# Where a pair's state products are issued, and GpSimd's order in the second pair

## The chip, the cores and the metric

The kernel runs on one core of a Trainium2 chip. The metric is the device time of one execution, in microseconds; times given for a kernel are medians over its runs. A core has TensorE (PE, matrix products into PSUM), VectorE (DVE), ScalarE (ACT), GpSimd (POOL) and SyncE (SP, which here only issues DMAs). Each engine works through its own list of instructions in order; semaphores make one engine wait for another.

## The reference, cut to what matters

Two blocks, one behind the other. The first is a state-space layer (Mamba-2's chunked form) over 4 sequences of 768 tokens with 8 heads of 32 channels and a state of 16; the second is a two-layer feed-forward block on the 3072 x 256 result, with 2048 hidden units and a parametric ReLU.

```python
for c in range(nc):
    L = np.exp(cum[:, :, :, None] - cum[:, :, None, :]) * causal
    M = np.einsum('bhin,bhjn->bhij', Cc, Bc) * L
    y_intra = np.einsum('bhij,bhjd->bhid', M, xc)
    y_inter = np.einsum('bhin,bhnd->bhid', Cc, state) * decay_to_i[:, :, :, None]
    y[:, :, sl] = y_intra + y_inter
    Bx = np.einsum('bhjn,bhjd->bhjnd', Bc, xc) * decay_from_j[:, :, :, None, None]
    state = decay_full[:, :, None, None] * state + np.sum(Bx, axis=2)
...
h = x @ w_in
g = np.maximum(h, 0.0) + alpha * np.minimum(h, 0.0)
return (g @ w_out).astype(np.float32)
```

The two weight matrices arrive as 64-bit floats; the kernel turns them into 32-bit floats itself, in pieces of 256 columns (`convert_a`, `convert_b`, `convert`).

## The kernel before, in words

**Pairs and groups.** The 24 chunks of 128 tokens are taken two at a time: 12 pairs, numbered 0 to 11. Two pairs make a group of 512 tokens, so there are 6 groups, and the feed-forward block works on groups. While the quads of group g run, pairs 2g + 2 and 2g + 3 are computed for the next group.

**A pair** is a Python generator (`pair`, L418); each call of `ssm(gp)` (L917) lets it issue its next stage. Its steps are: transposes of B and C (L511) and ScalarE's copy of them (`bc`); the decays, by scans on DVE (`half_decays`, L438, and `decays`, L427); C spread for the heads (`spread_c`, ScalarE) and C times the running decay (`c_decayed`, L528, POOL, tile `cd`); the state additions `added` (L473, PE, L478); the new states `states` (L483: DVE L490, then the heads' mask on POOL, L493, tile `sm`); the Gram products of B and C (`products_bc`, L573, PE, L580), in four strips r of 32 rows that run side by side, two of them into `ss` tiles and, for r = 2 and 3, into the two `hp` tiles; the multiplication of decays and Gram products on DVE (L614; in pairs 0 and 1 two heads of it are done by POOL, `times`, L591); the outputs (L633 and L640, PE); and two copies of them on ScalarE (L649). Pairs from 4 on are called fine: their scans and products are cut into more stages. B is scaled ahead by POOL (`pair_loads`, L379, tile `bn`).

**Quads.** Groups 1 to 5 use a scheme with seven half-size products in place of eight, in both layers. A group has four quads, z = 0 to 3, and there are 20 quads, i = 0 to 19 (`quad`, L773). A quad computes hidden units in two `hp` tiles, A and Y, by seven products (L785), each of two instructions and so four rows of the trace: A1, Y1, A2, Y2 and so on, in this order: A (copied by ScalarE to m1), Y (copied to m5), A again (copied to u2), then A, Y, then A for g21 and, last, Y for g11. Before the last one ScalarE copies m1 into Y (L814), after g12 was read from it. The parametric ReLU (`prelu`, L764) is a ScalarE product (L768) and a DVE maximum (L770). POOL then forms differences of the blocks (L819, L828). Between its products a quad calls `after(j)`, steps j = 1 to 14, and all else is hung into these steps by tables: the stages of the pairs (`steps`), the output products (`product`, L749, PE L760, numbered 1 to 7, each of four rows and of two halves of two) of the quad before it, combining a finished group's products (`combine`, L837), sums of weights (`weight_sums`, L728), and B's scaling for coming pairs. Even quads (z = 0 and 2) that have a pair beside them hold the Gram products in step 13; odd ones hold the outputs in step 5. The first quad (i = 0) has no output products of a quad before it, and in their place those of group 0 (L699).

**Before the quads.** Pairs 0 and 1 are computed alone; from about 30 us on, group 0 goes through the feed-forward block in the plain way (`hidden`, L656, `output`, L693) while pairs 2 and 3 are computed and the weights are converted. `slopes` (L306, POOL, L308 to L317) derives the factors of the parametric ReLU, and `hidden_two` (L668) starts group 0's hidden units with half a group.

The order on every engine is the program's order, written out by hand: `manual_schedule` takes it as it stands, and tile pools set which buffer is reused.

Of the kernel before, what the change touches and what calls it, by code (L numbers as in the profile page):

```python
# [22 lines left out]
def kernel(  # L23
# [25 lines left out]
    nc = tc.nc  # L49
# [279 lines left out]
    beside = {}  # L329

# [87 lines left out]
    def pair(gp):  # L418
# [4 lines left out]
        fine = gp >= 2 * GC // 2  # L423
# [43 lines left out]

        nk = 1 if last else 2
        st = [masked.get(b)]
        new = work.tile([P, 2, P], F32, name="state")  # L470
        sm = work.tile([P, 2, P], F32, name="sm")

        def added(dps):  # L473
            dps = dps[:, : 2 * Q].rearrange("p (k m) -> p k m", m=P)
            for k in range(nk):
                for w in range(KC):
                    ws = slice(64 * w, 64 * w + 64)
                    nc.tensor.matmul(dps[ws, k], bn[:, k, ws], xt[:, k, w * P : (w + 1) * P],  # L478
                                     start=True, stop=True, tile_position=(0, 64 * w),
                                     skip_group_check=True)  # L480
            return dps

        def states(dps):  # L483
            for k in range(nk):
                old = state.get(b)
                if old is None:
                    nc.scalar.copy(out=new[:, k], in_=dps[:, k])
                else:
                    e = (k + 1) * Q - 1
                    nc.vector.scalar_tensor_tensor(out=new[:, k], in0=old, scalar=pf[:, e : e + 1],  # L490
                                                   in1=dps[:, k], op0=ALU.mult, op1=ALU.add)
                state[b] = new[:, k]
            nc.gpsimd.tensor_tensor(out=sm[:, :nk], in0=new[:, :nk],  # L493
                                    in1=hmask.unsqueeze(1).to_broadcast([P, nk, P]), op=ALU.mult)
            st.extend(sm[:, k] for k in range(nk))
            masked[b] = st[-1]

        if fine:
            bn = bns.pop(gp) if gp in bns else pair_loads(gp)
            dps = added(beside.pop(gp) if gp in beside else ss_tile()[:, : 2 * Q])  # L500
            yield
            states(dps)
            yield


# [25 lines left out]

        if gp < 2:
            spread_c()
# [6 lines left out]
        if not fine:  # L540
            bn = bns.pop(gp) if gp in bns else pair_loads(gp)
# [6 lines left out]

        if fine:
            for k in range(2):  # L550
                for w in range(2):
                    half_decays(k, w)
                    if k == 1 and w == 1:
                        spread_c()
                        c_decayed()
                    yield
        else:
            if gp > 1:
                states(added(ss_tile()))
                c_decayed()  # L560
            decays(0)
            if gp == 1:
                dps = added(dps)
            if gp:
                yield
            if gp != 1:
                decays(1)
            if gp > 1:
                spread_c()
# [30 lines left out]
        elif gp == 1:  # L600
            gram = products_bc()
            g0 = one_less(gram)
            yield
            decays(1)
            states(dps)
            times(dec[:, :, :2], g0)
        else:
            if not fine:
                yield
            gram = products_bc()  # L610
# [11 lines left out]
        ys = [ss_tile() for w in range(KC)]  # L622
        y = [t[:, : 2 * Q].rearrange("p (k t) -> p k t", k=2) for t in ys]
        if fine:
            beside[gp + 1] = ys[1][:, 2 * Q :]
# [17 lines left out]
        if fine:  # L643
            yield
# [104 lines left out]
    def product(g, z, n, parts=(0, 1)):  # L749

        if g not in ms:
# [4 lines left out]
        for p in parts:  # L756
# [212 lines left out]
    ssm(1)  # L969
    slopes(alpha)  # L970
    ssm(1)
    prelus = [hidden_two(0, 0, 0, spare())]
    convert_next(first=False)
# [17 lines left out]
    for f in range(FIRST, NF):  # L991
# [12 lines left out]
        if f == 14:  # L1004
            bns[4] = pair_loads(4)
# [7 lines left out]
        if f in in_steps:  # L1013
# [3 lines left out]
    ssm(2 * GC // 2, 4)  # L1017


    steps = {(0, 1): 0, (0, 2): 0, (0, 5): 0, (0, 13): 0, (1, 1): 0, (1, 5): 0,  # L1020
             (1, 12): 1, (1, 14): 1, (2, 1): 1, (2, 2): 1, (2, 5): 1, (2, 13): 1,
# [12 lines left out]

    with_gram = {5: ((1,), (2, (0,))), 7: ((2, (1,)), (3,)), 8: ((5, (0,)),), 11: ((5, (1,)), (7,)),
                 13: ((6,),), 14: ((4,),)}
    without = {3: ((1,),), 5: ((2,),), 7: ((3,),), 8: ((5,),), 9: ((7,),), 13: ((6,),), 14: ((4,),)}
    for i in range(NZ * (NG - 1)):
# [3 lines left out]
        def after(j, g=g, z=z, i=i, nxt=nxt):  # L1042
            places = with_gram if nxt < NP and z % 2 == 0 else without
            for n in places.get(j, ()) if i else ():
                product(*divmod(NZ + i - 1, NZ), *n)
# [7 lines left out]
            if g > 1 and z == 0 and j in (7, 11, 13, 14):  # L1053
                if j == 7:
                    comb[0] = combine(g - 1)
# [3 lines left out]
            if nxt + steps.get((z, j), NP) < NP:  # L1059
                ssm(nxt + steps[z, j])  # L1060

                if j == 5 and z % 2:
                    for p in (1, 0, 1):
                        if nxt + z // 2 + p < NP:
                            ssm(nxt + z // 2 + p)
            if nxt < NP and (z, j) == (3, 7):
                token_sums(g + 1)
            ahead = nxt + {(0, 9): 1, (2, 9): 2}.get((z, j), NP)
# [42 lines left out]
```

## Time and profile before

| | |
|---|---|
| time, median of 4 runs | 373.26 us (372.25 to 373.66) |
| profiled execution, its own time | 373.12 us |
| profiled execution, span of the core | 371.0 us |
| PE busy | 363.7 us |
| DVE, ACT, POOL busy | 246.1, 179.5, 201.2 us |
| TensorE clock granted | 1.0 |

The page of a profile gives each engine's busy time, the chain of work that ended last, and the costliest groups of instructions. A row of a timeline has the start in us, the length in us, the engine, the line of the program, the operation, its tiles (written <- read), its shape and how many instructions were merged (x8); in brackets, how long the engine had been idle and what ended that. A wait list has engine, tile and line, whom it waited for, and then the sum in us, the number and the longest. PE rows overlap: a 128x256 row is 0.38 us long, and the next starts 0.216 us after it.

### The profile page before, as it was taken

The numbers are of one execution on the slowest core, as the hardware profiler recorded it, in microseconds if no ns is written. First come the engines' busy times: TensorE is split into PE (matmuls) and PEld (weight loads), VectorE is DVE, ScalarE is ACT, GpSimd is POOL, SyncE is SP. The second block draws the span as 40 slices with busy tenths as digits, with TensorE's granted clock in tenths as the row PEclk, the third lists the DMA queues.
The fourth block names the chain that finished last, engine by engine and source line by source line (L and its number), as shares of the span: only waits on it lengthen the run. The fifth ranks groups of instructions, "written<-read, shape, count | busy, mean of one in ns | idle before, by whom it ended". The sixth has DMA issues, their size and how long they took to land.

```text
span 371.0 us, 6171 instructions
## 1 busy us (share of the span) xinstructions
PE 363.7 (98%) x2223; PEld 292.0 (79%) x2223; DVE 246.1 (66%) x462; ACT 179.5 (48%) x384; POOL 201.2 (54%) x211
## 2 busy tenths in 40 slices
PE   8989999999999999999999999999999999999996
PEld 7766666578788888788788788788788788888884
DVE  7897979968448647838638738638747644643364
ACT  2647866436345345444444545446436425553541
POOL 4875566779738755725636526437445345264512
PEclk9999999999999999999999999999999999999999
DMA  8889999902175301004603702801801001001004
GB/s 163 178 166 317 266 269 220 193 10 58 42 143 103 82 3 57 2 0 74 140 3 58 155 2 48 167 0 35 177 3 29 2 0 28 4 0 30 0 0 85
DMA packets 121877, 30.71 MB, mean 83 GB/s; under 512 B 93736, under 2 KB 117752, under 8 KB 121848
## 3 DMA queue, kind: packets, MB, share of 16 engines
q1 hardware_dynamic: 116736, 29.74, 35.8%
q10 hardware_dynamic: 5112, 0.59, 1.1%
q8 instruction: 17, 0.28, 0.3%
q14 instruction: 12, 0.10, 0.1%
HBM read 26.98 MB, written 3.34 MB: 82 GB/s over the span
## 4 chain that ended last, share of the span: by engine, by line
PE 92%; DVE 2%; DMA 2%; POOL 1%; ACT 1%; issue 0%; ACTq 0%; POOLq 0%
PE hp L785 34%; PE bank L760 33%; PE bank L699 7%; PE hp L661 6%; PE ss L640 3%; PE ss L580 2%; PE ss L633 2%; PE ss L478 1%; PE ss L511 1%; PE hp L676 1%; DMA raw<-in_moe_w_in_dram 1%; DMA nat<-in_B_dram 1%; DVE dec L435 1%; PE bank L580 1%; PE bank L640 1%; DVE gt L770 0%
## 5 line engine op out<-in xcount | busy, mean ns | idle before, releaser
L828 POOL TENSOR_TENSOR gt<-gt 128x512 f32<-128x512 f32 x58 | 73.6, 1270 | 38.3 <-DVE gt L770 31.6
L760 PE MATMUL bank<-gt,w_out 128*128 128x256 f32 x320 | 82.4, 381 | 0.0
L770 DVE SCALAR_TENSOR_TENSOR gt<-hp,s_mul,gt 128x256 f32<-128x256 f32 x120 | 52.5, 479 | 43.5 <-ACT gt L768 40.8
L768 ACT ACTIVATE gt<-hp,s_alpha 128x256 f32<-128x256 f32 x120 | 50.3, 470 | 48.8 <-PE hp L785 36.6
L760 PEld LDWEIGHTS bank<-gt,w_out 128*128 128x128 f32 x320 | 60.1, 190 | 10.4 <-issue 2.3
L760 PE MATMUL bank<-gt,ws 128*128 128x256 f32 x240 | 59.5, 379 | 0.0
L819 POOL TENSOR_TENSOR gt<-gt 128x512 f32<-128x512 f32 x20 | 25.4, 1271 | 57.0 <-DVE gt L770 56.6
L760 PEld LDWEIGHTS bank<-gt,ws 128*128 128x128 f32 x240 | 45.1, 190 | 5.8
L441 DVE TENSOR_TENSOR_SCAN dec<-abc,bank 128x256 f32<-128x256 f32 x80 | 48.0, 660 | 0.0
L785 PE MATMUL hp<-xs,w_in 128*128 128x256 f32 x160 | 42.3, 387 | 0.0
L785 PE MATMUL hp<-xT,w_in 128*128 128x256 f32 x160 | 41.9, 384 | 0.1
L785 PE MATMUL hp<-xs,ws 128*128 128x256 f32 x160 | 40.7, 382 | 0.0
L793 ACT COPY m<-hp 128x512 f32<-128x512 f32 x20 | 11.7, 586 | 52.5 <-PE hp L785 47.4
L804 DVE TENSOR_TENSOR hp<-hp,u 128x512 f32<-128x512 f32 x20 | 13.9, 693 | 34.5 <-ACT u L802 34.5
L785 PEld LDWEIGHTS hp<-xT,w_in 128*128 128x128 f32 x160 | 29.1, 190 | 7.2 <-ACT hp L814 2.9
L785 PEld LDWEIGHTS hp<-xs,ws 128*128 128x128 f32 x160 | 29.8, 190 | 5.5 <-issue 1.1
L785 PEld LDWEIGHTS hp<-xs,w_in 128*128 128x128 f32 x160 | 29.3, 190 | 6.1 <-issue 1.2
L699 PE MATMUL bank<-w_out,gt 128*128 128x256 f32 x128 | 31.0, 384 | 0.0
L699 PEld LDWEIGHTS bank<-w_out,gt 128*128 128x128 f32 x128 | 23.7, 190 | 6.6 <-issue 3.7
L493 POOL TENSOR_TENSOR sm<-state,bmask 128x256 f32<-128x256 f32 (+1 forms) x12 | 7.8, 654 | 35.2 <-DVE state L490 35.0
L661 PE MATMUL hp<-xT,w_in 128*128 128x512 f32 x48 | 22.8, 597 | 0.2 <-DVE gt L688 0.2
L770 DVE SCALAR_TENSOR_TENSOR gt<-c,s_mul,gt 128x256 f32<-128x256 f32 x40 | 20.7, 559 | 0.0
(156 smaller groups left out, 550.2 us busy)
## 6 DMA issues: line engine op xcount, KB each, us to landing
abc<-z SPq DMA_DIRECT2D x20, 512.0 KB, 4.8
raw<-in_moe_w_in_dram SPq DMA_DIRECT2D x8, 512.0 KB, 5.6
raw<-in_moe_w_out_dram SPq DMA_DIRECT2D x8, 512.0 KB, 6.3
xt<-in_x_dram SPq DMA_DIRECT2D x24, 128.0 KB, 2.7
out_dram<-o_sb SPq DMA_DIRECT2D x32, 64.0 KB, 1.9
nat<-in_B_dram SPq DMA_DIRECT2D x22, 64.0 KB, 3.5
nat<-in_C_dram SPq DMA_DIRECT2D x22, 64.0 KB, 2.8
ap<-pf SPq DMA_DIRECT2D x11, 128.0 KB
```

The costliest lines, as they stand in the source:

```text
L441: nc.vector.tensor_tensor_scan(out=dv[:, k, hs], data0=abc[k][:, hs], data1=ident_p[0], initial=0.0, op0=ALU.mult, op1=ALU.add)
L640: nc.tensor.matmul(y[w][32 * q : 32 * q + 32, k], xt[:, k, h * D : (h + 1) * D], dec[:, k, h], start=False, stop=True, tile_position=(0, 3 ...
L661: nc.tensor.matmul(hp, w_in[:, k, f * P : (f + 1) * P], xts[g][:, k], start=(k == 0), stop=(k == KC - 1))
L699: nc.tensor.matmul(pos[0][t // 2][:, t % 2], gt[:, t * Q : (t + 1) * Q], w_out[:, f], start=(f == 0 and t % 2 == 0), stop=(f == NF - 1), s ...
L760: nc.tensor.matmul(ms[g][i][:, h], w, blocks[g, z][n][:, p], start=(q == 0 and h == 0), stop=(q == NQ - 1), skip_group_check=True)
L768: nc.scalar.mul(o[:, p], h[:, p], s_alpha[:, fs[p]])
L770: nc.vector.scalar_tensor_tensor(out=o[:, p], in0=h[:, p], scalar=s_mul[:, fs[p]], in1=o[:, p], op0=ALU.mult, op1=ALU.max)
L785: nc.tensor.matmul(to[:, p], w(2 * z + p), b, start=start and p == 0, stop=True, skip_group_check=True)
L793: nc.scalar.copy(out=m1, in_=A)
L804: nc.vector.tensor_tensor(out=Y, in0=Y, in1=u2, op=ALU.add)
L819: nc.gpsimd.tensor_tensor(out=tc_, in0=g22, in1=g12, op=ALU.subtract)
L828: eng.tensor_tensor(out=o, in0=x0, in1=x1, op=ALU.subtract)
```

## The change

Nothing is added to the computation or taken from it; instructions change places.

- In fine pairs the state additions (L478) and the states (L490, mask L493) were stages of their own at the head of a pair, called in the step of an odd quad that also has the outputs of the pair before (step 5). Their result went beside that pair's outputs, into the second half of a `ss` tile, and the outputs' copies were a stage behind. Now they are the stage before the Gram products, which a new entry of `steps` calls in step 9 of the even quad, into a `ss` tile of their own; `cd` is computed with them rather than with the last scans; and the copies follow the outputs at once.
- In even quads with a pair, product 1 goes back from step 5 to step 3, product 2 stands whole in step 5, 3 in step 7, 5 whole in step 8, and 7 in step 11.
- `combine` takes steps 5, 9, 13, 14 rather than 7, 11, 13, 14. B's scaling is called in steps (1, 3) and (3, 8) rather than (0, 9) and (2, 9), and pair 4's in its own first stage. Pair 4 has two stages ahead of the first quad rather than four.
- In pair 1, POOL's `times` goes ahead of `states`, and the third stage of the pair and the conversion of the second weight piece (whose last part is POOL's addition, L261) go ahead of `slopes`.

```diff
-        if fine:
-            bn = bns.pop(gp) if gp in bns else pair_loads(gp)
-            dps = added(beside.pop(gp) if gp in beside else ss_tile()[:, : 2 * Q])
-            yield
-            states(dps)
-            yield
...
         if fine:
             for k in range(2):
                 for w in range(2):
                     half_decays(k, w)
                     if k == 1 and w == 1:
                         spread_c()
-                        c_decayed()
                     yield
...
             decays(1)
+            times(dec[:, :, :2], g0)
             states(dps)
-            times(dec[:, :, :2], g0)
         else:
-            if not fine:
-                yield
+            if fine:
+                states(added(ss_tile()))
+                c_decayed()
+            yield
             gram = products_bc()
...
-        ys = [ss_tile() for w in range(KC)]
-        y = [t[:, : 2 * Q].rearrange("p (k t) -> p k t", k=2) for t in ys]
-        if fine:
-            beside[gp + 1] = ys[1][:, 2 * Q :]
+        y = [ss_tile()[:, : 2 * Q].rearrange("p (k t) -> p k t", k=2) for w in range(KC)]
...
-        if fine:
-            yield
         g, q = divmod(2 * gp, GC)
...
     ssm(0)
     ssm(1)
+    ssm(1)
+    convert_next(first=False)
     slopes(alpha)
-    ssm(1)
     prelus = [hidden_two(0, 0, 0, spare())]
-    convert_next(first=False)
     ssm(1)
...
-        if f == 14:
-            bns[4] = pair_loads(4)
...
-    ssm(2 * GC // 2, 4)
+    ssm(2 * GC // 2, 2)
-    steps = {(0, 1): 0, (0, 2): 0, (0, 5): 0, (0, 13): 0, (1, 1): 0, (1, 5): 0,
-             (1, 12): 1, (1, 14): 1, (2, 1): 1, (2, 2): 1, (2, 5): 1, (2, 13): 1,
+    steps = {(0, 1): 0, (0, 2): 0, (0, 5): 0, (0, 9): 0, (0, 13): 0, (1, 1): 0, (1, 5): 0,
+             (1, 12): 1, (1, 14): 1, (2, 1): 1, (2, 2): 1, (2, 5): 1, (2, 9): 1, (2, 13): 1,
              (3, 1): 1, (3, 5): 1, (3, 12): 2, (3, 14): 2}
...
-    with_gram = {5: ((1,), (2, (0,))), 7: ((2, (1,)), (3,)), 8: ((5, (0,)),), 11: ((5, (1,)), (7,)),
-                 13: ((6,),), 14: ((4,),)}
-    without = {3: ((1,),), 5: ((2,),), 7: ((3,),), 8: ((5,),), 9: ((7,),), 13: ((6,),), 14: ((4,),)}
+    with_gram = {3: 1, 5: 2, 7: 3, 8: 5, 11: 7, 13: 6, 14: 4}
+    without = {3: 1, 5: 2, 7: 3, 8: 5, 9: 7, 13: 6, 14: 4}
...
-            if g > 1 and z == 0 and j in (7, 11, 13, 14):
-                if j == 7:
+            if g > 1 and z == 0 and j in (5, 9, 13, 14):
+                if j == 5:
                     comb[0] = combine(g - 1)
...
-                if j == 5 and z % 2:
-                    for p in (1, 0, 1):
-                        if nxt + z // 2 + p < NP:
-                            ssm(nxt + z // 2 + p)
...
-            ahead = nxt + {(0, 9): 1, (2, 9): 2}.get((z, j), NP)
+            ahead = nxt + {(1, 3): 1, (3, 8): 2}.get((z, j), NP)
```

## The prediction

> **What bounds the kernel now.** I read the page's busy shares first, then the shares of the chain that ended last, then TensorE's waits, then the timelines around one pair. The first two:
>
> ```profile
> PE 363.7 (98%) x2223; PEld 292.0 (79%) x2223; DVE 246.1 (66%) x462; ACT 179.5 (48%) x384; POOL 201.2 (54%) x211
> ...
> PE 92%; DVE 2%; DMA 2%; POOL 1%; ACT 1%; issue 0%; ACTq 0%; POOLq 0%
> ```
>
> TensorE (PE) is busy in 363.7 of 371.0 us and carries 92% of the chain. GpSimd (POOL), whose order is changed, costs time only where PE waits for it. Three of PE's waits, as its wait list has them:
>
> ```profile
> PE hp L676 <- DVE state L490: 1.3, 1, 1.3
> ...
> PE ss L633 <- POOL sm L493: 0.5, 1, 0.5
> ...
> PE hp L580 <- DVE gt L770: 0.2, 1, 0.2
> ```
>
> The first lies in pair 1 at 22 us, the second in pair 0, the third in the first quad. Asked for 33 to 358 us alone, the list has only the third. So there is little to gain by removing waits in the quads; time can be lost by making them, or by lengthening PE's own stream. The list leaves out stalls that are shorter; the spacing of PE's rows shows them. Four 128x256 rows take 0.86 us (0.216 each); more than that is a stall or a change between whole-array and tiled products. An even quad in which a pair has its Gram products (group 2, z = 2), PE and then VectorE (DVE):
>
> ```profile
> 177.12 1.03 PE L785 MATMUL hp<-xs,w_in 128*128 128x256 f32 x4
> 178.12 1.13 PE L785 MATMUL hp<-xT,w_in 128*128 128x256 f32 x4
> 179.09 0.59 PE L760 MATMUL bank<-gt,ws 128*128 128x256 f32 x2
> ...
> 180.38 1.03 PE L760 MATMUL bank<-gt,ws 128*128 128x256 f32 x4
> 181.34 0.48 PE L580 MATMUL ss<-cz,bc 32*128 32x256 f32 x2
> ...
> 182.41 1.13 PE L760 MATMUL bank<-gt,w_out 128*128 128x256 f32 x4
> ```
>
> ```profile
> 179.11 0.88 DVE L770 SCALAR_TENSOR_TENSOR gt<-hp,s_mul,gt 128x256 f32<-128x256 f32 x2 [0.94 <-ACT gt L768]
> 180.22 0.88 DVE L770 SCALAR_TENSOR_TENSOR gt<-hp,s_mul,gt 128x256 f32<-128x256 f32 x2 [0.23 <-ACT gt L768]
> ```
>
> The reader is to see three things. The last hidden product (178.12, into Y) starts 0.14 late after four rows at 177.12, and its four rows take 0.97, so 0.24 is lost there; the same place in z = 0 (205.61, 206.67, 207.64) loses 0.20 + 0.10. The Gram products start at 181.34, 0.10 after the product before them would end: the price of entering tiled mode. And Y is free for the fourth Gram strip when g11's second L770 ends, 181.10, which is 2.01 after Y's last row (179.09). PE came 0.2 later than that, so it did not wait.
>
> **The change part by part.** Both kernels issue the same instructions on every engine, and the same DMAs in the same order on SP's queue; what changes is where they stand.
>
> (1) Steps 3 to 14 of the even quads. Before, product 1 and half of 2 stand together in step 5, and half of product 5 is held back to step 11, so PE has ten rows between Y's last row and the Gram products (179.09 to 181.34). After, each product stands whole, and eight rows are left: 8 x 0.216 + 0.09 for the mode, and the fourth strip 0.02 behind the first: 1.84. Y's release is 2.01 away, and PE starts 0.06 behind it, as in the first quad, PE and DVE:
>
> ```profile
> 94.82 0.48 PE L580 MATMUL hp<-cz,bc 32*128 32x256 f32 x1 [0.16 <-DVE gt L770]
> ```
>
> ```profile
> 92.94 1.04 DVE L728 TENSOR_TENSOR w_out<-w_out 128x512 f32<-128x512 f32 x1
> 93.90 0.86 DVE L770 SCALAR_TENSOR_TENSOR gt<-hp,s_mul,gt 128x256 f32<-128x256 f32 x2
> ```
>
> (93.90 + 0.86 = 94.76, PE at 94.82). So the fourth strip waits 2.07 - 1.84 = 0.23, and all of that is lost, because from the fourth strip to the next product it is 1.06 there (94.82 to 95.88) as without a wait (181.35 to 182.41). Behind it in PE's queue stand the rest of the Gram products and product 4.
>
> Product 1 in step 3 now covers the copy of m1 that A's second product waits for (0.08 lost in z = 2 at 171.7, 0.145 in z = 0), but product 2 alone in step 5 covers the copy of u2 less, with the same 0.86 us for the same 0.59 us copy. I take these as equal: 0.
>
> (2) The state additions (L478) leave the place behind the outputs (L633, L640) and go between the last two hidden products of the next even quad. Where they were:
>
> ```profile
> 160.80 0.66 PE L478 MATMUL ss<-xt,bn 128*64 128x128 f32 x8
> ```
>
> The next row starts at 161.39, so they cost 0.59 (0.37 with four rows), and leaving saves that, since the outputs must leave tiled mode anyway. In the new place they cost the same and 0.09 to enter tiled mode and 0.10 behind it: +0.20. They also lie where PE lost 0.24 (z = 2) or 0.30 (z = 0): Y waited for ScalarE's copy L814, which ended at 178.07; PE now comes there at 177.98 + 0.68 = 178.66. That loss goes.
>
> The rows so show 0.09 in and 0.10 out. The Trainium skill, TensorEngine Tiling (Array Packing), section Key Properties, says that changing the tiling mode drains the array, which speaks against the move. Taken as a full drain, an estimate from that page and from a row's length of 0.38 against its spacing of 0.216, each change would be 0.16, and the sum over seven pairs 0.9 us worse.
>
> (3) The states' DVE additions (L490, 0.35 each, 0.73 for two) now stand between g21's and g11's L770, and the mask and the decayed C (0.73 each on POOL) before the subtractions L828. DVE has room: g21's L770 ends 2.01 after A's last row, the states 2.74 at most, and g11's L770 can't start before 0.68 + 0.97 + 1.13 = 2.78 (L478, Y's rows, ScalarE). Margin 0.04 with two additions, 0.4 with one: 0. POOL's L828 results are used a quad later, and the mask by the outputs some 5 us later: 0, covered by whole products in between.
>
> (4) Seven pairs (5 to 11): four in z = 2 at 0.23 + 0.20 - 0.24 = +0.19, three in z = 0 at 0.23 + 0.20 - 0.30 = +0.13: 0.76 + 0.39 = 1.15.
>
> (5) Pair 4 in the first quad: its L478 and L490 move from before the quad into it. PE starts the quad 0.68 earlier and gives that back. There the fourth strip waits for DVE, which has L728 (1.04) too. Chain: A's last row 91.07 - 0.68 = 90.39; Y's 92.04; on DVE g21 to 92.3, states to 93.03, L728 to 94.0, g11 to 94.86; PE at 94.92 in place of 94.82: +0.10. The bounds are -0.2 (PE's own stream) and +0.7 (all of L490 in the way).
>
> (6) Combining a group's products two steps earlier puts a 0.37 copy and a 0.43 addition of group 2 to 5 in step 5, where ScalarE and DVE wait for PE anyway; B's scaling (L387) moves a step or so. 0 each; without cover 0.4 in four quads.
>
> (7) Pair 1, at 20 us. POOL, as it was, and PE:
>
> ```profile
> 18.82 0.31 POOL L308 TENSOR_SCALAR over<-alpha 128x16 f32<-128x16 f32 x1
> 19.21 0.67 POOL L309 TENSOR_SCALAR s_mul<-over 128x16 f32<-128x16 f32 x1
> ...
> 20.58 1.27 POOL L261 TENSOR_TENSOR w_in<-wr,wg 128x512 uint32<-128x512 uint32 x1
> 22.77 0.74 POOL L493 TENSOR_TENSOR sm<-state,bmask 128x256 f32<-128x256 f32 x1 [0.92 <-DVE state L490]
> 23.45 1.28 POOL L592 TENSOR_TENSOR dec<-o_sb,dec 128x512 f32<-128x512 f32 x1
> ```
>
> ```profile
> 22.83 1.97 PE L676 MATMUL hp<-xT,w_in 128*128 128x256 f32 x8 [1.33 <-DVE state L490]
> ...
> 25.16 0.37 PE L633 MATMUL bank<-cd,sm 64*128 64x128 f32 x1
> ```
>
> L261 needs DVE's L239, done at 19.81, so it runs 19.87 to 21.14. The slopes follow: as long as before (18.82 to 20.62, 1.8) they end at 22.94, then L592 to 24.2 and the mask to 24.95. The outputs start at 25.16: margin 0.2. PE's wait of 1.33 ended on the states (DVE, 22.70), which do not move, so the earlier weights gain nothing. The first prelu's slope comes at 22.5 and its ScalarE row at 22.5 in place of 21.60, ahead of DVE's use at 24.40. I take 0; the bounds are -0.5 (DVE's L238 takes 0.93 there and 0.45 elsewhere, beside POOL's work) and +0.5 (the mask late).
>
> L309 took 0.67 beside DVE's L238 and L239, the like L317 0.25 without them. The Trainium skill, SBUF — State Buffer, section Who interferes with whom, says that VectorE and GpSimd lock each other out of a shared pair of ports in some forms. By the rule the slopes would take some 1.3 in the new place, beside scans, an estimate from that page and these rows; the sum would be the same, with a margin of 0.7.
>
> Sum: 1.15 + 0.10 = +1.25 us, against the profiled run (span 371.0, time 373.12): span 372.3. That run is 0.14 under the median of 373.26, so the median becomes **374.5**.
>
> **Rivals.** *Deeper waits*: two state additions have only 0.04 of room, and one addition 0.35 more would show if L478 came late; with it in seven pairs (2.5) the time is 377.0, with it in half of them and 0.5 in pair 1 it is 376.0. For it: VectorE's chain has no slack left. Against: single additions have 0.4.
> *Not slower*: Y's release keeps ahead of the fourth strip. It decides if PE reaches the strip 0.23 later than I counted, for which a stall of A's products on the u2 copy does not help (it comes earlier), but a mode change of 0.2 more would. Then the sum is 1.25 - 7 x 0.23 = -0.36: 372.9.
> *The early order pays*: if DVE's scans and states in pair 1 come 0.5 earlier once the slopes are gone from beside L238, or the wait of 1.33 was partly for the weights after all, up to 1.3 goes, and with the not-slower case 371.6; alone 373.2. For it: L238's 0.93. Against: POOL's cd runs beside it either way.
> *The change does nothing for pair 1*, though it is named for it: this is in my forecast.
>
> **How the numbers follow.** About 0.3% (1.1 us) is what a measurement of this kernel can tell from no change. Forecast, 0.52, own range 373.9 to 375.4: 0.42 slower, 0.10 same. Deeper waits, 0.16: slower. Not slower, 0.18: 0.13 same, 0.05 faster. Early gain, 0.14: 0.11 faster, 0.03 same. Sums: faster 0.16, same 0.26, slower 0.58. The range runs from 372.3, inside the early gain, to 376.0, half way into the deeper waits, with about 1 in 10 left out on either side.
>
> **What would show it.** Right: seven rows "hp L580 waits for gt L770" of 0.1 to 0.3; no late start of the last hidden product; L478 alone between L785 rows, 0.2 dearer; PE at 22.8 and 25.2 us as before. Wrong: no L580 waits, or PE's outputs in pair 1 waiting for the mask, or the 1.33 wait shorter.

## The result, and the profile after

The changed kernel takes 373.65 us (median of 42 runs, 372.77 to 374.81), the kernel before 373.06 (64 runs in turn with it). The ratio is 1.0015, with a 95% interval of 1.001 to 1.002: half a microsecond slower. I had predicted +1.25 us and 374.5. The time lies in the predicted range, below the forecast's own 373.9 to 375.4, and by my own bound of 0.3% it is no change, to which I had given 0.26, not the "slower" that I held likeliest.

The profiled execution of the changed kernel took 373.53 us, its span is 371.6. In its lines the additions L478 are L520, the states L490 are L532, the mask L493 is L535, the Gram products L580 are L570, the ReLU's L770 is L757, the hidden products L785 are L772, the output products L760 are L747, and the weight sum L728 is L715. Busy times and the chain's shares, from its page:

```profile
PE 364.3 (98%) x2223; PEld 293.8 (79%) x2223; DVE 243.4 (65%) x462; ACT 179.4 (48%) x384; POOL 200.2 (54%) x211
...
PE 93%; DVE 3%; DMA 1%; ACTq 1%; issue 0%; ACT 0%; POOLq 0%; DVEq 0%
```

PE is as much the bound as before. PE's wait list of the changed kernel, two of its rows:

```profile
PE hp L663 <- DVE state L532: 1.0, 1, 1.0
...
PE ss L622 <- POOL sm L535: 0.2, 1, 0.2
```

There is no row for the Gram products (L570) at all, although the strips do wait, as the spacing shows. So I split the span by the starts of the pairs' outputs (the first row of L633, or L622 after), which both kernels have:

| stretch | before | after | difference |
|---|---|---|---|
| start to the outputs of pair 1 | 25.16 | 24.98 | -0.18 |
| pair 1 to pair 4 (holds the first quad) | 76.96 | 76.50 | -0.46 |
| pair 4 to pair 11 (the seven pairs of the sum) | 199.87 | 201.06 | +1.19 |
| pair 11 to PE's last row | 65.77 | 65.77 | 0 |

The seven pairs give +0.20, +0.23, +0.18, +0.12, +0.17, +0.12 and +0.17 (their even quads are z = 2 and 0 by turns). A quad of one of them, the one of the prediction (group 2, z = 2), PE and then VectorE, after:

```profile
176.76 1.03 PE L772 MATMUL hp<-xs,w_in 128*128 128x256 f32 x4
177.72 0.66 PE L520 MATMUL ss<-xt,bn 128*64 128x128 f32 x8
178.31 1.13 PE L772 MATMUL hp<-xT,w_in 128*128 128x256 f32 x4
179.27 1.03 PE L747 MATMUL bank<-gt,w_out 128*128 128x256 f32 x4
...
181.09 0.48 PE L570 MATMUL ss<-cz,bc 32*128 32x256 f32 x2
181.11 0.71 PE L570 MATMUL hp<-cz,bc 32*128 32x256 f32 x2
...
182.39 1.13 PE L747 MATMUL bank<-gt,w_out 128*128 128x256 f32 x4
```

```profile
179.55 0.72 DVE L532 SCALAR_TENSOR_TENSOR state<-state,ap,ss 128x128 f32<-128x128 f32 x2
180.40 0.88 DVE L757 SCALAR_TENSOR_TENSOR gt<-hp,s_mul,gt 128x256 f32<-128x256 f32 x2
```

The additions stand between the last two hidden products. 0.96 lies from the product before them to their first row, and 0.97 from the next product to the row behind it, where four rows take 0.86: the two changes, into tiled products and out of them, cost 0.09 and 0.10. Y's release is the end of VectorE's last row, 180.40 + 0.88 = 181.28. The Gram products begin at 181.09, and the row of 0.71 is two merged rows of 0.48, so the fourth strip starts at 181.11 + 0.71 - 0.48 = 181.34, 0.23 behind the others. From the first strip to the next product it is 1.30, in place of 1.07 before (181.34 to 182.41).

The first quad went the other way. PE there, before:

```profile
93.96 0.48 PE L580 MATMUL ss<-cz,bc 32*128 32x256 f32 x2
...
95.88 1.99 PE L699 MATMUL bank<-w_out,gt 128*128 128x256 f32 x8
```

PE, VectorE and GpSimd there, after:

```profile
93.63 0.48 PE L570 MATMUL ss<-cz,bc 32*128 32x256 f32 x2
...
95.25 1.99 PE L686 MATMUL bank<-w_out,gt 128*128 128x256 f32 x8
```

```profile
92.66 0.69 DVE L715 TENSOR_TENSOR w_out<-w_out 128x512 f32<-128x512 f32 x1
93.27 0.87 DVE L757 SCALAR_TENSOR_TENSOR gt<-hp,s_mul,gt 128x256 f32<-128x256 f32 x2
```

```profile
92.89 1.04 POOL L535 TENSOR_TENSOR sm<-state,bmask 128x256 f32<-128x256 f32 x1 [1.24 <-DVE state L532]
```

The Gram products there take 1.62 to the next product, in place of 1.92 before (93.96 to 95.88), though VectorE has the states to do as well. That is -0.30 of the -0.46; PE also starts the quad (the transposes, L511 and L469) 0.68 earlier, counted from the outputs of pair 1, since the additions are gone from there, and is 0.53 longer from there to the Gram products. VectorE's weight sum took 0.69 instead of 1.04. This time the sum began first, at 92.66, and GpSimd's mask, begun at 92.89, took 1.04 instead of its usual 0.73. Before, GpSimd had begun first with B's scaling, as its row in the kernel before says:

```profile
92.79 0.64 POOL L387 TENSOR_TENSOR bn<-nat,prt 128x256 f32<-128x256 f32 x1
```

and the sum, begun at 92.94, was the one that took 1.04.

Pair 1, GpSimd, after:

```profile
19.72 1.27 POOL L261 TENSOR_TENSOR w_in<-wr,wg 128x512 uint32<-128x512 uint32 x1 [1.57 <-DVE wr L239]
21.07 0.25 POOL L308 TENSOR_SCALAR over<-alpha 128x16 f32<-128x16 f32 x1
...
22.31 1.28 POOL L582 TENSOR_TENSOR dec<-o_sb,dec 128x512 f32<-128x512 f32 x1
23.55 0.73 POOL L535 TENSOR_TENSOR sm<-state,bmask 128x256 f32<-128x256 f32 x1
```

The mask ends at 24.28, and the outputs start at 24.98. From VectorE's second scan of pair 1 (its row at 19.73 before, 19.56 after) to the outputs it is 5.43 us in both kernels. The -0.18 is already there when that scan starts.

### The profile page after: what moved, and what is told of

It reads as the page before. It is cut to its first block, busy times and chain, and to the rows that moved or that the text cites. A ratio compares the mean times of both kernels' runs of the same rounds, so it can differ in the third digit from the quotient of the medians.

```text
span 371.6 us, 6184 instructions
## 1 busy us (share of the span) xinstructions
PE 364.3 (98%) x2223; PEld 293.8 (79%) x2223; DVE 243.4 (65%) x462; ACT 179.4 (48%) x384; POOL 200.2 (54%) x211
## 4 chain that ended last, share of the span: by engine, by line
PE 93%; DVE 3%; DMA 1%; ACTq 1%; issue 0%; ACT 0%; POOLq 0%; DVEq 0%
PE hp L772 34%; PE bank L747 32%; PE bank L686 8%; PE hp L648 6%; PE ss L629 3%; PE ss L570 2%; PE ss L622 1%; PE ss L520 1%; DMA nat<-in_B_dram 1%; DVE dec L432 1%; PE hp L570 1%; PE ss L469 1%; PE hp L663 1%; PE bank L629 0%; PE hp L270 0%
## 5 line engine op out<-in xcount | busy, mean ns | idle before, releaser
L757 DVE SCALAR_TENSOR_TENSOR gt<-hp,s_mul,gt 128x256 f32<-128x256 f32 x120 | 52.5, 479 | 46.8 <-ACT gt L755 45.8
L747 PE MATMUL bank<-gt,w_out 128*128 128x256 f32 x320 | 82.4, 381 | 0.0
L747 PEld LDWEIGHTS bank<-gt,w_out 128*128 128x128 f32 x320 | 60.1, 190 | 10.4 <-issue 2.3
L747 PE MATMUL bank<-gt,ws 128*128 128x256 f32 x240 | 58.3, 379 | 0.0
L747 PEld LDWEIGHTS bank<-gt,ws 128*128 128x128 f32 x240 | 45.1, 190 | 5.8
L772 PE MATMUL hp<-xs,w_in 128*128 128x256 f32 x160 | 42.8, 390 | 0.0
L772 PE MATMUL hp<-xT,w_in 128*128 128x256 f32 x160 | 41.9, 384 | 0.0
L772 PE MATMUL hp<-xs,ws 128*128 128x256 f32 x160 | 41.1, 379 | 0.0
L772 PEld LDWEIGHTS hp<-xs,w_in 128*128 128x128 f32 x160 | 28.7, 189 | 7.7 <-issue 3.0
L772 PEld LDWEIGHTS hp<-xs,ws 128*128 128x128 f32 x160 | 30.4, 190 | 4.1
L772 PEld LDWEIGHTS hp<-xT,w_in 128*128 128x128 f32 x160 | 29.7, 190 | 5.0 <-issue 1.4
L795 DVE TENSOR_TENSOR c<-hp,m 128x512 f32<-128x512 f32 x20 | 13.6, 682 | 19.3 <-PE hp L772 19.3
L648 PE MATMUL hp<-xT,w_in 128*128 128x512 f32 x48 | 22.8, 598 | 0.2 <-DVE gt L675 0.2
L789 ACT COPY u<-hp 128x512 f32<-128x512 f32 x20 | 11.7, 585 | 22.5 <-PE hp L772 22.5
```

Source lines behind the costliest of these rows:

```text
L648: nc.tensor.matmul(hp, w_in[:, k, f * P : (f + 1) * P], xts[g][:, k], start=(k == 0), stop=(k == KC - 1))
L747: nc.tensor.matmul(ms[g][i][:, h], w, blocks[g, z][n][:, p], start=(q == 0 and h == 0), stop=(q == NQ - 1), skip_group_check=True)
L757: nc.vector.scalar_tensor_tensor(out=o[:, p], in0=h[:, p], scalar=s_mul[:, fs[p]], in1=o[:, p], op0=ALU.mult, op1=ALU.max)
L772: nc.tensor.matmul(to[:, p], w(2 * z + p), b, start=start and p == 0, stop=True, skip_group_check=True)
L795: nc.vector.tensor_tensor(out=c22, in0=A, in1=m5, op=ALU.add)
```

## The experiments

My theory: a quad pays for the strip wait (half of product 5 no longer held back) and for two mode changes, and gains the late start of the last hidden product; the first quad gains from the order in which VectorE and GpSimd began; pair 1 is off the path. The rivals: the early order of pair 1 pays or costs; the strip wait and the late start are one loss of VectorE's chain, seen in two places; moving the additions costs more than its mode changes. The table has each run's median, its ratio to the kernel before on the same chip, and two stretches of its profile, found as above.

| kernel | median us | ratio (95%) | pair 1 to 4 | pair 4 to 11 |
|---|---|---|---|---|
| before | 373.06 to 373.22 | | 76.96 | 199.87 |
| changed | 373.65 | 1.0015 (1.001 to 1.002) | 76.50 | 201.06 |
| pair 1's order alone | 373.65 | 1.0013 (1.0003 to 1.0024) | 78.25 | 199.91 |
| changed, half of 5 held back | 373.15 | 1.0002 (0.9991 to 1.0014) | 76.30 | 200.23 |
| changed, pair 1 as before | 373.86 | 1.0024 (1.0014 to 1.0034) | 76.97 | 201.05 |
| changed, half of 5 held back, sum later | 372.77 | 0.9989 (0.9981 to 0.9998) | 76.19 | 200.23 |
| before, products whole | 374.34 | 1.0033 (1.0020 to 1.0046) | 77.26 | 201.38 |
| before, half of 2 moved to step 7 | 372.93 | 0.9987 (0.9978 to 0.9997) | 77.27 | 199.70 |
| before, sum later | 372.37 | 0.9978 (0.9967 to 0.9990) | 76.31 | 199.85 |
| before, both of these | 372.16 | 0.9969 (0.9957 to 0.9980) | 76.31 | 199.70 |
| additions as cover | 371.39 | 0.9958 (0.9942 to 0.9973) | 76.19 | 199.51 |
| the same, pair 1 as before | 371.94 | 0.9965 (0.9953 to 0.9978) | 75.98 | 199.51 |

The stretch from pair 4 to 11 is the same within 0.06 in kernels with the same seven quads, so it tells a tenth of a microsecond. The stretch from 1 to 4 is not so steady: two kernels that differ in nothing there lie 0.3 apart (before, and half of 2 moved: 76.96, 77.27). All of that lies ahead of the first quad. From the last row of group 0's output products ahead of the quad (80.83 before) to the outputs of pair 4 it is 21.29 or 21.30 in the four kernels whose first quad is that of the kernel before, 20.83 in the three that have the changed one, 20.66 in the two of the kernel before with the sum later, and 20.51 or 20.52 in the three with both. So the -0.46 belongs to the first quad.

### The seven pairs: one term at a time

**Half of product 5 held back.** The changed kernel with this:

```diff
-    with_gram = {3: 1, 5: 2, 7: 3, 8: 5, 11: 7, 13: 6, 14: 4}
+    with_gram = {3: ((1,),), 5: ((2,),), 7: ((3,),), 8: ((5, (0,)),), 11: ((5, (1,)), (7,)), 13: ((6,),), 14: ((4,),)}
...
```

> The changed kernel, with half of product 5 put back from step 8 to step 11 in even quads, and nothing else: two rows of 0.216 us move from before the last hidden product to behind it. Theory (the fourth Gram strip waits for Y): PE reaches the strip 0.43 us after it did, counted from Y's last row, and the Gram products take 1.07 us again in place of 1.30; seven quads at 0.23 us make 1.6 us, less up to 0.25 us in each of the z = 0 quads whose last hidden product then waits for ScalarE's copy: 1.0 to 1.6 us faster than the changed kernel, about 372.3 us, under both kernels. Rival: the last hidden product starts late again by what is gained, in all quads, and the time is that of the changed kernel within 0.3 us.

In this kernel, and in the one below that is made from it, the second step of combining copies product 5 of the group before ahead of its second half, so that step computes something else; the work is the same. Seven pairs: 200.23, 0.83 less than in the changed kernel, and the median is 0.5 less. The 0.83 is half of the 1.6 that the strips alone would give. The Gram products show the strip wait gone, PE in the same quad:

```profile
181.14 0.48 PE L570 MATMUL ss<-cz,bc 32*128 32x256 f32 x2
181.16 0.48 PE L570 MATMUL hp<-cz,bc 32*128 32x256 f32 x2
...
182.22 1.13 PE L747 MATMUL bank<-gt,w_out 128*128 128x256 f32 x4
```

It is 1.08 now, and 0.48 is one length for all strips. But something comes back, most in z = 0 with one addition; PE and ScalarE of this kernel there:

```profile
206.00 0.44 PE L520 MATMUL ss<-xt,bn 128*64 128x128 f32 x4
206.54 1.13 PE L772 MATMUL hp<-xT,w_in 128*128 128x256 f32 x4
```

```profile
205.90 0.59 ACT L801 COPY hp<-m 128x512 f32<-128x512 f32 x1 [0.23 <-DVE gt L757]
```

The last hidden product starts 0.54 after the additions, 0.37 in the changed kernel (206.61 to 206.98): it waits again for ScalarE's copy into Y, which ends at 206.49. The half that went behind Y as cover for the strip was, ahead of Y, cover for the copy. In the two quads of z = 2 with one addition 0.06 and 0.11 come back so, with two additions 0.01 at most. And in every quad of z = 0 the held-back half waits 0.10 more: its two rows take 0.54 in place of 0.43 (207.57 to 208.10), behind combining's copy of its bank, which ends at 207.52. That wait is this edit's own.

**The products whole, the additions left where they were.** The kernel before with the other part alone:

```diff
-    with_gram = {5: ((1,), (2, (0,))), 7: ((2, (1,)), (3,)), 8: ((5, (0,)),), 11: ((5, (1,)), (7,)),
-                 13: ((6,),), 14: ((4,),)}
+    with_gram = {3: ((1,),), 5: ((2,),), 7: ((3,),), 8: ((5,),), 11: ((7,),), 13: ((6,),),
+                 14: ((4,),)}
```

> The kernel before with one part of the change alone: in even quads with a pair, product 1 stands in step 3, 2 in step 5, 3 in step 7, 5 whole in step 8, 7 in step 11; the state additions stay behind the outputs. My theory (the strip wait is lost time of its own): eight rows instead of ten lie between Y's last row and the Gram products, so each of seven pairs has Gram products of 1.30 in place of 1.07, and the late start of the last hidden product stays at 0.24 and 0.30: 7 x 0.23 = +1.6 us, about 374.7. Rival (the strip wait is only the other face of a chain through VectorE, which the late start or the strip pays once): the quad loses less than 0.1 each and the time is at most 373.8.

Seven pairs: 201.38, +1.51, where I expected +1.6; the median is 1.1 higher. PE of this kernel in the same quad:

```profile
178.62 1.03 PE L785 MATMUL hp<-xs,w_in 128*128 128x256 f32 x4
179.62 1.13 PE L785 MATMUL hp<-xT,w_in 128*128 128x256 f32 x4
...
182.41 0.48 PE L580 MATMUL ss<-cz,bc 32*128 32x256 f32 x2
182.43 0.71 PE L580 MATMUL hp<-cz,bc 32*128 32x256 f32 x2
...
183.71 1.13 PE L760 MATMUL bank<-gt,w_out 128*128 128x256 f32 x4
```

Both losses stand in one quad: 1.00 between the last two hidden products, where four rows take 0.86 (the late start), and 1.30 for the Gram products (the strip wait). So the strip wait is a loss of its own, and the rival of one loss in two places falls for this pair of places. The difference to the changed kernel is what moving the additions does by itself: 201.06 - 201.38 = -0.32, where my terms say 4 x -0.04 + 3 x -0.10 = -0.46. In the changed kernel 0.11 of that is something else: with B's scaling moves one transpose on PE (L370, L368 after). Before it stood at 120.80 in the gap of a late start; now it stands at 135.37, in the second of the seven pairs, where it covers nothing and costs 0.11.

**More cover for the late start.** The kernel before with half of product 2 in step 7 instead of step 5:

```diff
-    with_gram = {5: ((1,), (2, (0,))), 7: ((2, (1,)), (3,)), 8: ((5, (0,)),), 11: ((5, (1,)), (7,)),
+    with_gram = {5: ((1,),), 7: ((2,), (3,)), 8: ((5, (0,)),), 11: ((5, (1,)), (7,)),
```

> The kernel before with half of product 2 moved from step 5 to step 7 in even quads with a pair, nothing else: two rows (0.43) more lie ahead of the last hidden product, where it starts 0.24 late (z = 2) or 0.30 late (z = 0); the rows behind it, ten, stay. Theory (the late start is a loss of its own): it goes in seven pairs, 4 x 0.24 + 3 x 0.30 = 1.9, and the product after the u2 copy, with four rows of cover instead of six, stalls 0.08 (z = 2) or 0.14 (z = 0) as in the changed kernel, 0.7 in all: -1.1 us, about 372.0, with Gram products still 1.07. Rival (the chain through VectorE sets the quad's length): the time comes back as a strip wait, Gram products of 1.2 to 1.3, and the time stays within 0.3 of the kernel before.

Seven pairs: 199.70, -0.17 where I expected -1.1; the ratio of 0.9987 is as small. The late start is gone, and the Gram products keep 1.08, so the rival of a strip wait was wrong too. The time went to a third place, earlier in the quad; PE and VectorE of this kernel:

```profile
173.28 1.11 PE L785 MATMUL hp<-xs,w_in 128*128 128x256 f32 x4
174.31 1.13 PE L785 MATMUL hp<-xT,ws 128*128 128x256 f32 x4
```

```profile
170.13 3.54 DVE L441 TENSOR_TENSOR_SCAN dec<-abc,bank 128x256 f32<-128x256 f32 x6
173.59 0.67 DVE L804 TENSOR_TENSOR hp<-hp,u 128x512 f32<-128x512 f32 x1
```

The product into Y at 174.31 follows VectorE's addition of u2 into Y, which ends at 174.26; that addition stands behind six scans of the pair. In the kernel before the same product came at 174.53 and did not wait, since two more rows stood ahead of it. From the first product of step 5 to the first of step 7 it is 2.87 here (172.41 to 175.28) with two rows less, 3.02 before (172.37 to 175.39): two rows are 0.43, so 0.28 is lost again, against the 0.24 gained; in z = 0 it is 0.22 against 0.30. Rows taken from one wait of this quad open another.

**Additions as that cover.** The additions L520 are rows from outside the quad. The changed kernel with the output products and the steps of combining as before, and VectorE's sum in step 11 (below):

```diff
-    with_gram = {3: 1, 5: 2, 7: 3, 8: 5, 11: 7, 13: 6, 14: 4}
+    with_gram = {5: ((1,), (2, (0,))), 7: ((2, (1,)), (3,)), 8: ((5, (0,)),), 11: ((5, (1,)), (7,)),
+                 13: ((6,),), 14: ((4,),)}
...
-            if g > 1 and z == 0 and j in (5, 9, 13, 14):
-                if j == 5:
+            if g > 1 and z == 0 and j in (7, 11, 13, 14):
+                if j == 7:
```

> The changed kernel (state additions between the last two hidden products, the new order in pair 1) with the output products and the steps of combining placed as in the kernel before (products 2 and 5 in halves), and VectorE's sum in step 11 of the first quad. Theory (my terms add): no strip wait, since ten rows lie behind Y's last row; 0.20 for the two mode changes, against a late start of 0.24 (z = 2) or 0.30 (z = 0) that goes: seven pairs 4 x -0.04 + 3 x -0.10 = -0.5 us against the kernel before, and -0.65 in the first quad as with the sum moved alone: about 372.0. Rival (moving the additions costs more than its mode changes, as the +0.36 of seven pairs in the kernel with half of product 5 held back would say): seven pairs +0.3 and the time 372.8.

371.39, ratio 0.9958 (0.9942 to 0.9973): the fastest of all, 1.8 us under the kernel before. Seven pairs: 199.51, -0.36, where the terms say -0.46 and the rival +0.3; the moved transpose is in it with 0.11, and the pairs without it, but for the first, gain 0.04 to 0.05 in z = 2 and 0.10 in z = 0, as the terms have it. PE in the same quad:

```profile
175.02 1.03 PE L772 MATMUL hp<-xs,w_in 128*128 128x256 f32 x4
175.97 0.66 PE L520 MATMUL ss<-xt,bn 128*64 128x128 f32 x8
176.56 1.13 PE L772 MATMUL hp<-xT,w_in 128*128 128x256 f32 x4
...
179.78 0.48 PE L570 MATMUL ss<-cz,bc 32*128 32x256 f32 x2
...
180.86 1.13 PE L747 MATMUL bank<-gt,w_out 128*128 128x256 f32 x4
```

Neither the late start (0.59 from the additions to the next product is their own time) nor the strip wait (1.08) is left. Of the 1.8 us, 0.36 is in the seven pairs and 0.77 between pairs 1 and 4; the remaining 0.7 lies ahead of pair 1's outputs (24.43, 25.16 before), where the runs scatter, as the last part shows. So 1.1 us can be put down to the edits.

### The first quad

**The sum behind the last ReLU.** The kernel before with this:

```diff
-                 (0, 10): ((wqt, out_sums, 0, 3, nc.vector),), (1, 2): ((wi, in_sums, 4, 1),),
+                 (0, 11): ((wqt, out_sums, 0, 3, nc.vector),), (1, 2): ((wi, in_sums, 4, 1),),
```

> The kernel before with VectorE's sum of output weights in the first quad moved from step 10 to step 11, so behind the last parametric ReLU instead of ahead of it. Theory (in the first quad the fourth Gram strip waits for that ReLU, and the sum of 1.04 us is what makes it late): the Gram products of the first quad, 1.92 from the first strip to the next product, take about 1.3, and the time falls by 0.6 to 372.5; the seven other pairs are as before. Rival (the strip waits for ScalarE's half of the ReLU or for TensorE anyway): they stay at 1.8 or more and the time stays.

PE, VectorE and GpSimd of this kernel in the first quad:

```profile
93.67 0.48 PE L580 MATMUL ss<-cz,bc 32*128 32x256 f32 x2
...
94.97 1.99 PE L699 MATMUL bank<-w_out,gt 128*128 128x256 f32 x8
```

```profile
93.78 0.68 DVE L728 TENSOR_TENSOR w_out<-w_out 128x512 f32<-128x512 f32 x1
```

```profile
93.94 3.00 POOL L828 TENSOR_TENSOR gt<-gt 128x512 f32<-128x512 f32 x2 [0.78 <-DVE gt L770]
```

The Gram products take 1.30, as expected, and the stretch of pairs 1 to 4 is 0.65 shorter; the median is 0.85 lower. So the sum was what made the strip late. It is also the same sum that now begins first (93.78) and takes 0.68, and GpSimd's two subtractions beside it take 3.00 in place of 2.62.

The two edits in one kernel:

> The kernel before with both edits: half of product 2 in step 7, and VectorE's sum in step 11. Theory: they lie in different quads and add up, -1.1 and -0.6: 371.4. Rival: if the first quad's wait and the late starts are paid back at the end of the quads, less than half of that shows, 372.4 or more.

372.16 (ratio 0.9969), where I expected 371.4: the stretch of pairs 1 to 4 is that of the one kernel, 76.31, and of pairs 4 to 11 that of the other, 199.70. They do not disturb each other, and nearly all of the gain is the sum's, since the cover gives only 0.17.

The sum in step 11 of the changed kernel with half of product 5 held back:

> As the kernel with half of product 5 later, and in the first quad VectorE's weight sum (L728 of the kernel before) one step later, behind the last maximum for g11. Theory: in the first quad the fourth strip waited 0.56 us because VectorE had the states and the sum ahead of g11's maximum; without the sum there it waits 0 to 0.1, and the time is 0.4 to 0.6 us under that kernel's, about 371.8 us. Rival: the sum then holds up the multiplications of the Gram products and the next quad's first product waits for what was gained: the same time within 0.2 us.

372.77, 0.38 under the kernel without that edit, a little less than expected; the Gram products of the first quad take 1.30. VectorE and GpSimd there:

```profile
94.14 1.12 DVE L715 TENSOR_TENSOR w_out<-w_out 128x512 f32<-128x512 f32 x1
```

```profile
93.30 0.73 POOL L535 TENSOR_TENSOR sm<-state,bmask 128x256 f32<-128x256 f32 x1 [1.23 <-DVE state L532]
93.98 0.72 POOL L487 TENSOR_TENSOR cd<-bc,ap 128x256 f32<-128x256 f32 x1
```

Now the mask, with no sum beside it, takes 0.73, and the sum, begun while GpSimd's `cd` runs, takes 1.12. In all these rows the one that begins first keeps its time, and the other is 0.3 to 0.45 longer. No kernel is an exception: the sum took 0.68 to 0.69 in the five in which it began first, and 1.04 to 1.12 in the seven in which GpSimd did.

### Pair 1's order

The kernel before with both parts of the new order and nothing else:

```diff
             decays(1)
+            times(dec[:, :, :2], g0)
             states(dps)
-            times(dec[:, :, :2], g0)
...
-    slopes(alpha)
     ssm(1)
-    prelus = [hidden_two(0, 0, 0, spare())]
     convert_next(first=False)
+    slopes(alpha)
+    prelus = [hidden_two(0, 0, 0, spare())]
```

> The kernel before, with pair 1's GpSimd order alone taken from the change (the second weight piece's addition ahead of the slopes, the heads' multiplication ahead of the states' mask). Theory: the slopes no longer run beside VectorE's sign step L238, which took 0.93 us before and 0.40 after, so VectorE's chain and with it the whole kernel comes 0.2 to 0.5 us earlier: 0.05 to 0.15% faster. Rival: the 0.18 us between the two profiles at 31 us is the input loads' scatter, and the time is that of the kernel before within 0.1 us. In the profile the theory has L238 at 0.4 to 0.55 us in pair 1, and PE's wait for the states at 22 us shorter than 1.33 us.

It was 0.56 us slower than the kernel before. Its profile, of the slowest of its twelve runs (374.80), puts 1.29 of loss between pairs 1 and 4, and none behind. PE's wait list and VectorE's timeline of this kernel:

```profile
PE hp L661 <- DVE gt L665: 1.1, 2, 0.6
```

```profile
56.17 0.51 DVE L341 TENSOR_SCALAR r<-rows 96x128 f32<-96x128 f32 x1 [2.35 <-DMA rows<-in_a_dram]
```

VectorE stood 2.35 us behind a load of decays 30 us after pair 1 (1.31 before, where its row starts at 54.42), and the ReLU of group 0 behind it. The load's issue on SP's queue took 3.51 us, 0.78 before. Is that the order's doing? The opposite edit, the changed kernel with the old order:

> The changed kernel with pair 1's old GpSimd order. Theory: 0.2 to 0.5 us slower than the changed kernel, that is 0.2 to 0.3% slower than the kernel before. Rival: the time of the changed kernel.

373.86: 0.2 slower than the changed kernel, with intervals that overlap. Here the old order had the slow issue, 2.95 us. And the fastest kernel with the old order in pair 1:

> The same kernel with GpSimd's order in pair 1 as before (slopes first, the heads' multiplication behind the states' mask). Theory (GpSimd lies off the path in pair 1): from VectorE's second scan of pair 1 to the outputs it is 5.43 us as in the kernels with either order, and the two times agree within 0.3. Rivals: the new order pays (this one is 0.3 to 0.5 slower), or it costs (0.3 to 0.5 faster), as the two runs with the order changed alone would say in opposite ways.

371.94 against 371.39, 0.55 slower. So one comparison says that the new order costs 0.56, and two that it saves 0.2 and 0.55. Only the first has an interval (1.0003 to 1.0024) that excludes no difference; those of the other two comparisons overlap. The traces side with none of them: in all twelve kernels the outputs of pair 1 start 5.42 or 5.43 us after VectorE's second scan, with either order. Ahead of that scan stands L238, which the theory of the first run had shorter without the slopes beside it. GpSimd and VectorE there, before and then after:

```profile
18.01 0.73 POOL L529 TENSOR_TENSOR cd<-bc,ap 128x256 f32<-128x256 f32 x1 [0.91 <-DMA ap<-pf]
18.09 0.93 DVE L238 TENSOR_SCALAR wr<-raw 128x512 uint32<-128x512 uint32 x1
```

```profile
17.42 0.72 POOL L487 TENSOR_TENSOR cd<-bc,ap 128x256 f32<-128x256 f32 x1
18.44 0.40 DVE L238 TENSOR_SCALAR wr<-raw 128x512 uint32<-128x512 uint32 x1
```

It is `cd` that lengthens L238, and not the slopes. In the seven kernels in which `cd` had waited for a load and had more than 0.1 us to go, two of them with the new order, L238 took 0.55 to 0.93 and ended 0.28 behind `cd`; in the other five, three of them with the new order, it took 0.40. So that theory was wrong, and this too is scatter of a load. The rest of what differs comes earlier or later. The slow issue is found with either order: 0.70 to 3.51 us in the five profiles with the new one, 0.78 to 2.95 in the seven with the old. PE's first transposes start between 7.1 and 8.6 us, by when the first loads land; between the last two kernels that is 7.83 and 8.54, and pair 1's outputs differ by the same 0.7 (24.43, 25.13); in the others the way from those transposes to the outputs varies as well, up to 17.9 us from 16.6 in these two. An effect of the order on the time is not shown; what these runs leave open is about half a microsecond either way.

## Why the prediction was right or wrong, by its steps

- **(1) Half of product 5, +0.23 per pair: right.** Alone it cost 1.51 in seven pairs, 0.22 each, and the fourth strip started 0.23 late where I said. Calling the copies' stalls equal held too: before, the first cover failed by 0.08 (z = 2) and 0.14 (z = 0), after it the second by the same in z = 2, and in z = 0 by 0.07 at each of two products.
- **(2) Additions, +0.20 and the late start gone: right within 0.14 in all.** The mode changes cost 0.09 and 0.10 in the rows, not the 0.16 each that the estimate from the Trainium skill (TensorEngine Tiling (Array Packing), Key Properties) gave; with it the seven pairs would have come to +2.0, and they came to +1.19. In the first of the seven the late start was 0.09 + 0.10 and not 0.24, since the transpose L370 stood in it.
- **(3) VectorE's states between two ReLUs, 0: right.** VectorE's row at 180.40 shows no strip later than 0.23, in z = 2 with two additions. The deeper waits did not come. (Their sum for half of the pairs and 0.5 in pair 1 is 374.5 + 1.2 + 0.5 = 376.2, where I wrote 376.0.)
- **(4) Seven pairs: +1.15 predicted, +1.19 measured.** By turns I had 0.19 and 0.13; it was 0.20, 0.23, 0.18, 0.12, 0.17, 0.12, 0.17, so only the second stands out, and that by the transpose of 0.11, which I had not counted. Without it the seven give 1.08, so that the sum came out as near as 0.04 is luck.
- **(5) First quad: wrong, +0.10 predicted, -0.46 measured, outside its bounds of -0.2 and +0.7.** The term that failed is "L728 to 94.0": I took the sum's 1.04 from a row that lay behind GpSimd's B scaling, while step (6) had that scaling moved away at a cost of nothing. In its new surroundings the sum took 0.69, 0.35 less. The rest of the error, 0.2, is in adding VectorE's durations, whose rows overlap by some 0.08 each: from g21's end to the strip I counted 92.3 to 94.92, 2.62, and it was 92.11 to 94.19, 2.08. The resource that the two engines share was not in the sum, although my own step (7) spoke of it for pair 1.
- **(6) Combining and B's scaling, 0: right for combining,** which nothing waited for. For B's scaling it is the miss of (5), and the 0.11 of the transpose that moves with it.
- **(7) Pair 1, 0: right as far as the runs tell.** The slopes took 1.28 in the new place (21.07 to 22.35) in place of 1.8, so the Trainium skill's rule (SBUF — State Buffer, Who interferes with whom), by which I had estimated 1.3, agrees, and the margin at the outputs was 0.7, not 0.2. PE came at 22.65 and 24.98 instead of 22.8 and 25.2, by a start that scatters. Two of my readings there were wrong: L309 (19.21 to 19.88) lay beside L239 alone, as L238 had ended at 19.02; and L238's 0.93, my bound of -0.5, came from `cd`, which the new order does not move.
- **What would show it:** I said that seven rows of 0.1 to 0.3 would appear in the wait list. None did. The list goes by PE's idle time, and while the fourth strip waits (until 181.34) the first rows of the other three still run (to 181.58), so PE is never idle; in the first quad of the kernel before it was, and there the list had its row. The spacing of PE's rows was the view to name.

The sum of the measured parts is -0.18 - 0.46 + 1.19 = +0.55, and the medians differ by 0.59. The mechanism for the seven quads was right, the sign of the whole was right, and the size was halved by one term, the first quad's. That the two sums agree to 0.04 is worth little, since the -0.18 is scatter of the start.

## What to carry to other kernels

When work moves, take its duration, and that of everything now beside it, from a row with the same neighbours; on VectorE and GpSimd it matters even which of two instructions begins first. In a stream that is 98% busy, rows moved from one gap to another mostly move the wait (three places in one quad did so here, for 0.17 us in seven pairs), while rows brought in from a place where they cover nothing fill it. Take each part of a change alone before judging it: this one was made of a small gain (the additions as cover, -0.3), a gain that I had not foreseen (the first quad, -0.46, with the sum begun first) and a larger loss (whole products, +1.5); with the products left in halves and the sum moved on purpose, the rest beats the kernel before, 371.39 against 373.17 us, of which 1.1 us lie in the stretches that were edited.

## What the runs showed of the hardware

- Of VectorE's sum, whose two inputs both lie in SBUF (0.68 to 0.69 where it began first), and a GpSimd product (0.73 alone) that overlap, the one that begins first keeps its time; the other took 1.04 to 1.12, and ended 0.55 to 0.58 after the first. The Trainium skill (SBUF — State Buffer, Who interferes with whom) says that a VectorE instruction with two SBUF inputs contends with a GpSimd instruction that reads SBUF. The rows agree, but the second was not blocked whole: some 0.15 of it ran beside the first, since its whole 0.73 or 0.69 behind the first would have ended later by that.
- From a whole-array row to the first tiled one it is 0.31 in place of 0.216, and four whole-array rows behind tiled ones take 0.97 in place of 0.86: 0.09 to 0.10 for the change at either end, in every kernel here, where no wait fell on it. The second figure is not the change's alone: four rows behind a wait take 0.97 as well (178.12 to 179.09 before).
- The start of a run scatters: the first transposes by 1.5 us (7.1 to 8.6), and the issue of one load near 48 us between 0.7 and 3.5 us, which the ReLU of group 0 sometimes waits for (up to 1.1 us). Differences of half a microsecond between medians of five to twelve runs can come from there, and the stretch behind pair 4, equal within 0.06 between like kernels, is the finer measure.
